# Attention and feed-forward block on one core: VectorE exps in groups of four tiles, an immediate exp bias, and measured times in the schedule model

## Chip, cores and metric

One NeuronCore of one Trainium2 chip. The metric is device time in microseconds (us) of one execution. Runs of one kernel agree within about 1.5% (the kernel before, over all its rounds: 1047.93 to 1064.23 us); every timed run here is in the fast state, except one single look, which has no state of its own and is marked. Ratios are the mean time of one kernel's runs over the mean of the kernel before's runs of the same rounds, so they are not quite the ratio of the medians that are quoted beside them.

Engine names in the profile: PE is TensorE (PEld its weight loads), ACT is ScalarE, DVE is VectorE, POOL is GpSimd.

## The reference

A pre-layernorm block: attention with 32 heads of width 16 over 2048 tokens of width 512, then a gated GELU layer of width 1792, both with residuals.

```python
q, k, v = split((layernorm(x) @ wqkv))           # 32 heads, Dh = 16
p = softmax(q @ k.T * Dh ** -0.5)                # 32 x 2048 x 2048 exps
h = x + (p @ v) @ wo
out = h + (gelu(layernorm(h) @ w_gate) * (layernorm(h) @ w_up)) @ w_down
```

The exps are the bulk: 2048 score tiles of 128 x 512.

## The kernel before

The program is built by a list scheduler that runs while the kernel is built. Every piece of work is an `Op` with an engine, a modelled duration, what it reads and what it writes. The scheduler keeps a modelled clock for each engine, always emits the op that can start first, and so fixes the **order** of instructions on each engine. On the chip, engines run their lists in that order and wait on semaphores. A wrong duration in the model costs no correctness; it gives an order in which an engine stands at an instruction whose input is late.

Attention runs in 40 units of four heads by 512 (in the last 16 units, 256) queries, with 64 (or 32) score tiles each. Q times K ("QK") fills PSUM banks 0 to 2 and 3 to 4 in turn. ScalarE turns three tiles and then two tiles into exps in the buffer `PT`. P times V ("PV") accumulates in bank 5. Banks 6 and 7 serve everything else: projections, the feed-forward layer, and score tiles whose exp VectorE computes instead of ScalarE.

```python
def _ready(self, op):                     # when the model lets an op start
    ...
    for k in op.reads:  r = max(r, self.done[P.last_writer[k]])
    ... # the same for the writers and readers of what it writes
    return r + LAT                        # LAT = 0.12, for every engine

def exps():                               # ScalarE, n = 3 or 2 tiles
    ...
    yield Op("act", 0.093 + 0.427 * n, ACTF(PT[:, p0:p0 + n, :], pbank[:, b0:b0 + n, :],
             ACT.Exp, scale=LN2 / 1024, bias=ebias[:]), ...)   # ebias: a 128x1 tile

def dexp(i, dn, b):                       # VectorE, one tile of 512 columns; [...] cut
    yield Op("dve", 0.66, tensor_scalar(out=X, in0=pbank[:, b, :], ...))   # conversion, frees the bank
    sch.release(b)
    yield Op("dve", 0.2,  tensor_scalar(out=M, in0=X, ...))    # mantissa
    yield Op("dve", 0.2,  tensor_scalar(out=E, in0=X, ...))    # power of two
    yield Op("dve", 0.33, tensor_tensor(out=W, in0=M, in1=M))
    yield Op("dve", 0.2,  tensor_scalar(out=W, in0=W, EK, EB))
    yield Op("dve", 0.33, tensor_tensor(out=W, in0=W, in1=M))
    yield Op("dve", 0.33, tensor_tensor(out=T, in0=W, in1=E))  # T; exp is E + T, by two matmuls

def pv():                                 # one step: four tiles, in order m = 0, 1, 2, ...
    for m in range(NT // r):
        yield Wait(lambda: all(4 * n + g in made for g in range(4)))
        ... # PE: PV of all four tiles; a VectorE tile takes two matmuls, with E and with T
```

## Time and profile before

Median of the first three runs 1058.76 us (1055.49 to 1060.64). From the ScalarE records I split the span as follows. "Exps" is the number of exps times their shortest start-to-start interval (1.423 us for three tiles, 0.997 for two). "Tanh" is 42 x 0.520 + 14 x 0.306. "Lost" is what remains between the first exp's start and the last exp's end. (Up to ten of the 256-wide tanhs start after the last exp, five of them in the kernel before, so "lost" is too low by up to 3 us.)

| us | head | exps | tanh | lost | tail after the last exp | span |
|---|---|---|---|---|---|---|
| before | 20.1 | 890.2 | 26.1 | 71.3 | 49.4 | 1057.0 |

From the page of the kernel before: busy time of each engine with its share of the span, then the costliest groups (line, engine, operation, tile written from tiles read, shapes, count; busy us, mean ns of one; idle time before them and what ended most of it).

```profile
PE 906.1 (86%) x7249; PEld 282.6 (27%) x7249; DVE 845.0 (80%) x1988; ACT 950.9 (90%) x830; POOL 200.0 (19%) x265
...
L1201 ACT ACTIVATE PT<-pbank,ebias 128x1536 bf16<-128x1536 f32 x736 | 912.5, 1398 | 51.8 <-PE pbank L1195 50.2
...
L1448 DVE TENSOR_SCALAR dX<-pbank 128x512 uint16<-128x512 f32 x208 | 142.2, 684 | 13.2 <-PE pbank L1195 12.7
...
L1455 DVE TENSOR_TENSOR dW<-dW,dM 128x512 f16<-128x512 f16 x208 | 102.1, 491 | 6.2
```

ScalarE is the busiest engine that cannot be relieved by waiting less: 912.5 of its 951 us are exps. (In a mixed group the shape named is the first one; the 736 exps are 368 of 1536 and 368 of 1024 columns.) VectorE spends seven instructions on each of 208 tiles, about 640 us.

The list of waits of the same kernel: who waited for whom, us in total, times, longest.

```profile
PEld pbank L1195 <- DVE dT L1457: 53.9, 85, 3.2
...
ACT PT L1201 <- PE pbank L1195: 50.2, 63, 3.1
PEld pbank L1194 <- DVE GUT L1630: 32.0, 30, 3.2
...
PE pbank L1195 <- DVE dT L1457: 25.1, 38, 2.7
```

PE stands 54 us at the weight load for `dT`, the last step of a VectorE exp, and ScalarE stands 50 us for PE. Three stretches of 50 us: busy time of each engine (with counts), the granted TensorE clock, DMA share, GB/s.

```profile
200.00:250.00 50.00, 43.34 (x311) 11.30 (x308) 45.77 (x124) 50.00 (x42) 0.00 (x0) 1.00 0.00 1
300.00:350.00 50.00, 40.54 (x255) 10.79 (x253) 40.96 (x71) 43.32 (x40) 26.25 (x25) 0.93 0.00 1
550.00:600.00 50.00, 37.36 (x207) 9.23 (x207) 44.46 (x76) 36.90 (x34) 23.64 (x23) 0.83 0.00 0
```

The first stretch has no feed-forward work (POOL at 0): ScalarE is busy without a gap. In the other two the feed-forward layer runs, and ScalarE falls to 43 and 37 of 50.

### The profile page before, as it was taken

To read this page: it belongs to the slowest core of one execution; us is meant where nothing else is said; L and a number is where in the kernel's file an instruction comes from. 1 tells how busy PE (TensorE), PEld (TensorE's weight loads), DVE (VectorE), ACT (ScalarE), POOL (GpSimd) and SP (SyncE) were. 2 spreads that over 40 slices of the span, in tenths; PEclk is the share of its full clock that TensorE was granted. 3 is DMA by queue.
4 is the path that set the end of the run, shared out by engine and by line. 5 is a ranking of instruction groups with operands and counts; after the bars stand their busy time and mean duration, and the time that the engine had idled before them with its cause. 6 is when DMAs were issued, how large, how long until landed. Compare 5 with 4: busy or idle time off the path is not lost.

```text
span 1057.0 us, 18656 instructions
## 1 busy us (share of the span) xinstructions
PE 906.1 (86%) x7249; PEld 282.6 (27%) x7249; DVE 845.0 (80%) x1988; ACT 950.9 (90%) x830; POOL 200.0 (19%) x265
## 2 busy tenths in 40 slices
PE   7999888888877799889887879988898878898877
PEld 2322222222212222222221222222233222333345
DVE  6457978998888989999778979999948898656853
ACT  6899999999988899999987888999999988999922
POOL 6300000000244410000033540000001454302340
PEclk8999999999999999999988899999999998999989
DMA  4000003200000001000000000100000000000000
GB/s 159 2 1 1 1 1 136 95 1 1 2 1 1 1 6 36 1 1 1 2 1 1 1 1 6 36 1 1 1 7 7 1 2 2 2 16 16 2 6 19
DMA packets 10769, 15.17 MB, mean 14 GB/s; under 512 B 688, under 2 KB 9136, under 8 KB 10672
## 3 DMA queue, kind: packets, MB, share of 16 engines
q1 hardware_dynamic: 10672, 13.90, 3.9%
q8 instruction: 59, 0.97, 0.4%
q14 instruction: 38, 0.31, 0.1%
HBM read 11.80 MB, written 2.10 MB: 13 GB/s over the span
## 4 chain that ended last, share of the span: by engine, by line
PE 28%; ACT 28%; DVE 28%; issue 14%; DMA 1%; SPq 0%; POOL 0%; ACTq 0%; DVEq 0%
ACT PT L1201 27%; PE pbank L1195 14%; PE pbank L1194 10%; DVE dW L1455 4%; PE pbank L1677 3%; DVE dT L1457 3%; DVE dX L1448 3%; DVE dW L1454 3%; DVE dW L1453 2%; DVE g_sb L1592 2%; DVE w_sb L1604 2%; DVE dM L1450 2%; DVE dE_57 L1451 2%; DVE QT L1332 2%; DVE GUT L1630 2%
## 5 line engine op out<-in xcount | busy, mean ns | idle before, releaser
L1201 ACT ACTIVATE PT<-pbank,ebias 128x1536 bf16<-128x1536 f32 x736 | 912.5, 1398 | 51.8 <-PE pbank L1195 50.2
L1195 PE MATMUL pbank<-QT,KT 32*128 32x512 bf16 (+1 forms) x2560 | 290.9, 344 | 74.5 <-ACT PT L1201 57.2
L1195 PE MATMUL pbank<-PT,VA 128*17 128x512 bf16 (+1 forms) x2312 | 206.2, 347 | 24.4 <-DVE dT L1457 21.7
L1195 PEld LDWEIGHTS pbank<-QT,KT 32*128 32x128 bf16 x2560 | 76.3, 91 | 353.6 <-ACT PT L1201 245.7
L1677 PE MATMUL pbank<-ones_bf,zero_bf 128*128 128x512 bf16 x483 | 153.7, 391 | 0.0
L1448 DVE TENSOR_SCALAR dX<-pbank 128x512 uint16<-128x512 f32 x208 | 142.2, 684 | 13.2 <-PE pbank L1195 12.7
L1555 POOL TENSOR_SCALAR rstd_105<-mv_104 128x1 f32<-128x1 f32 x16 | 3.8, 240 | 585.1 <-DVE mv_104 L1553 585.0
L1455 DVE TENSOR_TENSOR dW<-dW,dM 128x512 f16<-128x512 f16 x208 | 102.1, 491 | 6.2
L1457 DVE TENSOR_TENSOR dT<-dW,dE_57 128x512 bf16<-128x512 f16 x208 | 96.9, 466 | 6.0
L1594 POOL TENSOR_TENSOR w_sb<-g_sb 128x512 f32<-128x512 f32 (+1 forms) x56 | 56.6, 1011 | 213.2 <-DVE g_sb L1592 213.2
L1453 DVE TENSOR_TENSOR dW<-dM 128x512 f16<-128x512 f16 x208 | 90.5, 435 | 0.0
L1195 PEld LDWEIGHTS pbank<-PT,VA 128*17 128x17 bf16 x2312 | 52.5, 88 | 135.5 <-issue 64.4
L1195 PE MATMUL pbank<-dE_57,VA 128*17 128x512 bf16 (+1 forms) x248 | 82.2, 358 | 3.1 <-DVE dT L1457 3.1
L1195 PE MATMUL pbank<-dT,VA 128*17 128x512 bf16 (+1 forms) x248 | 81.7, 356 | 0.0
L1454 DVE TENSOR_SCALAR dW<-dW 128x512 f16<-128x512 f16 x208 | 71.9, 346 | 5.6
L1450 DVE TENSOR_SCALAR dM<-dX 128x512 uint16<-128x512 uint16 x208 | 67.6, 325 | 5.5
L1451 DVE TENSOR_SCALAR dE_57<-dX 128x512 uint16<-128x512 uint16 x208 | 68.2, 328 | 0.0
L1596 POOL TENSOR_TENSOR w_sb<-w_sb,g_sb 128x512 f32<-128x512 f32 (+1 forms) x56 | 67.1, 1198 | 4.7
L1677 PEld LDWEIGHTS pbank<-ones_bf,zero_bf 128*128 128x128 bf16 x483 | 39.3, 98 | 73.4 <-issue 62.2
L1194 PE MATMUL pbank<-wd_sb,GUT 128*128 128x512 bf16 x224 | 58.4, 382 | 0.2
L1592 DVE COPY g_sb<-pbank 128x512 f32<-128x512 f32 (+1 forms) x56 | 34.7, 620 | 20.7 <-PE pbank L1194 20.4
L1603 ACT ACTIVATE w_sb<-w_sb 128x512 f32<-128x512 f32 (+1 forms) x56 | 34.0, 607 | 13.3 <-POOL w_sb L1596 13.2
(126 smaller groups left out, 766.3 us busy)
## 6 DMA issues: line engine op xcount, KB each, us to landing
xres<-in_A_x_dram SPq DMA_DIRECT2D x16, 128.0 KB, 2.2
out_dram<-out_sb SPq DMA_DIRECT2D x16, 128.0 KB, 1.7
wg_sb<-in_B_w_gate_dram SPq DMA_DIRECT2D x1, 1792.0 KB, 7.0
wu_sb<-in_B_w_up_dram SPq DMA_DIRECT2D x1, 1792.0 KB, 11.5
wd_sb<-in_B_w_down_dram SPq DMA_DIRECT2D x1, 1792.0 KB, 16.6
x_sb<-in_A_x_dram SPq DMA_DIRECT2D x3, 512.0 KB, 10.3
wqkv_sb<-in_A_wqkv_dram SPq DMA_DIRECT2D x2, 768.0 KB, 8.7
x_sb<-in_A_x_dram SPq DMA_DIRECT2D x2, 256.0 KB, 3.9
```

The lines of the kernel that those rows point to most:

```text
L1194: return lambda e: e.matmul(o, l, r, start=start, stop=stop)
L1195: return lambda e: e.matmul(o, l, r, start=start, stop=stop, tile_position=tile)
L1201: return lambda e: e.activation(out=o, in_=i, func=func, **kw)
L1448: yield Op("dve", 0.66, lambda e: e.tensor_scalar(out=X, in0=pbank[:, b, :], scalar1=1024.0 * CENTER, scalar2=0.0, op0=ALU.add, op1=ALU.ma ...
L1450: yield Op("dve", 0.2, lambda e: e.tensor_scalar(out=M.bitcast(U16), in0=X, scalar1=0x3ff, scalar2=0x3c00, op0=ALU.bitwise_and, op1=ALU.bi ...
L1451: yield Op("dve", 0.2, lambda e: e.tensor_scalar(out=E.bitcast(U16), in0=X, scalar1=3, scalar2=0x1f80, op0=ALU.logical_shift_right, op1=AL ...
L1453: yield Op("dve", 0.33, lambda e: e.tensor_tensor(out=W, in0=M, in1=M, op=ALU.mult), reads=[kM], writes=[kW])
L1454: yield Op("dve", 0.2, lambda e: e.tensor_scalar(out=W, in0=W, scalar1=EK, scalar2=EB, op0=ALU.mult, op1=ALU.add), reads=[kW], writes=[kW])
L1455: yield Op("dve", 0.33, lambda e: e.tensor_tensor(out=W, in0=W, in1=M, op=ALU.mult), reads=[kW, kM], writes=[kW])
L1457: yield Op("dve", 0.33, lambda e: e.tensor_tensor(out=T, in0=W, in1=E, op=ALU.mult), reads=[kW, kE], writes=[kT])
L1596: yield Op("pool", 1.27, lambda e: e.tensor_tensor(out=ws, in0=ws, in1=gs, op=ALU.mult), reads=[("w", i), ("g", i)], writes=[("w", i)])
L1677: fill_op = Op("pe", TMM, lambda e: e.matmul(pbank[:, PVB, :], zero_bf[:], ones_bf[:], start=False, stop=False, skip_group_check=True), re ...
```

## The change

Intent: let VectorE do its exps in groups of four tiles (2048 columns an instruction, fewer fixed costs), take their PV products out of the ordered PV steps so that PE never waits for one tile, drop the bias pointer of the exp, and put measured times and a truer readiness rule into the schedule model. The core of the diff, with cuts marked:

```diff
     def _ready(self, op):
...
+            if op.eng == "pe":                       # PE no longer lags behind PE
+                lag = LAT + (SLACK if op.writes[0] in SOFT else 0.0)
+                return max([self.done[t] + lag for t in toks if t[0] != "pe"] + [0.0])
+            lag = LAT + (SLACK if op.eng == "act" and op.writes[0][0] == "w" else 0.0)
+            return max([self.done[t] + lag for t in toks] + [0.0])
...
+SLACK = 0.3
+SOFT = (("pb", 6), ("pb", 7))
-NRING = 25
+NRING = 20                                           # tiles in the ring PT
+GS = 4
+GLAST = 16
...
-    ... bias=ebias[:]
+    ... bias=-LN2 * (127 - CENTER) - math.log(EC)
...
+    def dconv(G, j, b):                              # once for each tile of a group
+        yield Op("dve", 0.7, ... tensor_scalar(out=dX[:, j, :], in0=pbank[:, b, :], ...
+    def dchain(G):                                   # once for each group, n tiles wide
+        t1, t2 = 0.16 + 0.133 * n, 0.16 + 0.267 * n
+        ... # three tensor_scalar of t1, three tensor_tensor of t2
...
     def pv():
+        # a group's products: one PE op, at any PV step of the unit once the group is done;
+        # the last PV step of a unit waits for all groups of the unit
```

A group may open only with at least 28 tiles (`GLAST + 12`) of the unit left, or in the last six tiles of the unit before, and only after the former group's chain has been issued but for its last instruction.

More of the change, by code (lines that the diff above doesn't have):

```diff
@@ L920, in _ready @@
         P = self.P
-        r = 0.0
+        toks = []
         for k in op.reads:
@@ L925, in _ready @@
                 return self.INF
-            r = max(r, self.done[tok])
+            toks.append(tok)
         if isinstance(op, Op):
@@ L930, in _ready @@
                 if tok is not None:
-                    r = max(r, self.done[tok])
-                for tok in P.readers.get(k, ()):
-                    r = max(r, self.done[tok])
-        return r + LAT
+                    toks.append(tok)
+                toks.extend(P.readers.get(k, ()))
+            if op.eng == "pe":
[3 more added lines that the diff above has]
+            return max([self.done[t] + lag for t in toks] + [0.0])
+        return max([self.done[t] + LAT for t in toks] + [0.0])
     def owed(self, t, n=0):
@@ L1035 @@
 F16, U16 = mybir.dt.float16, mybir.dt.uint16
-ND = 5
+GS = 4
+GLAST = 16
 DFROM = 20
-DGAP = 1.8
-DMAX = 8
+DGAP = 6.0
+DBUSY = 0.0
 LN2 = 0.6931471805599453
@@ L1103, in fast_path @@
     offX = cur[0]
-    dX = at("dX", [128, 2, 512], U16)
-    dM = at("dM", [128, 2, 512], F16)
-    dW = at("dW", [128, 2, 512], F16)
-    dE2 = at("dE2", [128, ND, 512], BF16)
-    dT = at("dT", [128, ND, 512], BF16)
-    ebias = at("ebias", [128, 1], FP32)
+    dX = at("dX", [128, GS, 512], U16)
+    dW = at("dW", [128, 2, GS, 512], F16)
+    dE2 = at("dE2", [128, 2, GS, 512], BF16)
     gset = at("gset", [128, 1], FP32)
@@ L1180, in fast_path @@
     TILES = [(u, m, g) for u in range(NU) for m in range(NT * CHUNKS[units[u][0]] // 512) for g in range(4)]
-    STEPS, own, made, acount = [], {}, set(), [0]
+    STEPS, own, made, groups = [], {}, set(), {}
     TUNIT = 0.88 * 64 * (0.093 * len(SLOTS) / sum(n for _, n in SLOTS) + 0.427)
     T0 = 12.0
+    unit0 = [sum(4 * NT * CHUNKS[c] // 512 for c, _ in units[:u]) for u in range(NU + 1)]
     sch = Sched(P, list(DENSE))
-    C = dict(exp=0, pv=0, oa=0, ln1=0, proj=0, oproj=0, gut=0, down=0, act=0, dbank=None, din=0, dn=0, dcons=0, dnext=0.0)
+    C = dict(exp=0, pv=0, oa=0, ln1=0, proj=0, oproj=0, gut=0, down=0, act=0, dbanks=[], gopen=None, gk=0, gw=0, gpv=0, acons=0, qpos=0, dnext=0.0)
     otok_n = {}
@@ L1227, in consts @@
         yield Op("pool", 0.1, lambda e: e.memset(zero_bf[:], 0.0), writes=["zero_bf"])
-        yield Op("pool", 0.1, lambda e: e.memset(ebias[:], -LN2 * (127 - CENTER) - math.log(EC)), writes=["ebias"])
         yield Op("pool", 0.3, lambda e: e.tensor_copy(out=ident32[:], in_=ident[:]), reads=["ident"], writes=["ident32"])
@@ L1358, in ffn_loads, with unit_of, pos_of @@
             yield Op("sp", 1.75, lambda e, o=o, i=i: e.dma_start(out=o, in_=i), writes=[nm], dma=nm, extra=lambda: dF)
+    def unit_of(i):
+        return TILES[i][0]
+    def pos_of(i):
+        u = unit_of(i)
+        return i - unit0[u], unit0[u + 1] - unit0[u]
     def qk():
-        nxt, an, dn = 0, 0, 0
+        nxt, an = 0, 0
         while nxt < len(TILES):
@@ L1365, in qk @@
             b0, n = SLOTS[st % len(SLOTS)]
-            n = min(n, len(TILES) - nxt)
-            STEPS.append((an, n, b0, nxt))
-            put = [(nxt + k, b0 + k) for k in range(n)]
-            for k in range(n):
-                own[nxt + k] = ("a", (an + k) % NRING)
-                acount.append(acount[-1] + 1)
-            nxt, an = nxt + n, an + n
-            d = None
-            db = C["dbank"]
-            if db is not None and nxt < len(TILES) - 12 and all(sch.done[t] <= sch.now + 0.7 for t in P.readers.get(("pb", db), ())):
-                d = (nxt, dn)
-                put.append((nxt, db))
-                own[nxt] = ("d", dn % ND)
-                acount.append(acount[-1])
-                nxt, dn = nxt + 1, dn + 1
-                C["dbank"] = None
+            mine = []
@@ new lines, in qk @@
+            while len(mine) < n and nxt < len(TILES):
+                if nxt not in own:
+                    own[nxt] = ("a", (an + len(mine)) % NRING)
+                    mine.append(nxt)
+                nxt += 1
+            STEPS.append((an, mine, b0))
+            put = [(i, b0 + k) for k, i in enumerate(mine)]
+            an += len(mine)
+            while nxt in own:
+                nxt += 1
+            C["qpos"] = nxt
+            G, late = C["gopen"], []
+            if G:
+                if nxt < len(TILES) and G["u"] is None and pos_of(nxt)[1] - pos_of(nxt)[0] >= GLAST + 12:
+                    G["u"] = unit_of(nxt)
+                used = {TILES[i][2] for i in mine}
+                while C["dbanks"] and len(G["t"]) < GS and len(put) < 4 and G["u"] is not None:
+                    db = C["dbanks"][0]
+                    if any(sch.done[t] > sch.now + 0.7 for t in P.readers.get(("pb", db), ())):
+                        break
+                    cand = [i for i in range(nxt, min(unit0[G["u"] + 1] - 8, nxt + 8)) if i not in own and TILES[i][2] not in G["g"] | used]
+                    if not cand:
+                        break
+                    i = cand[0]
+                    C["dbanks"].pop(0)
+                    own[i] = ("d", G["k"] % 2)
+                    late.append((i, len(G["t"]), db))
+                    G["t"].append(i)
+                    G["g"].add(TILES[i][2])
+                    used.add(TILES[i][2])
+                    put.append((i, db))
+                while nxt in own:
+                    nxt += 1
+                if len(G["t"]) == GS or nxt >= len(TILES) or (G["u"] is not None and (unit_of(nxt) != G["u"] or pos_of(nxt)[1] - pos_of(nxt)[0] <= GLAST)):
+                    close_group()
@@ L1396, in qk, with close_group @@
             C["qk"] = st + 1
-            if d:
-                sch.add(dexp(*d, db), 70000)
+            C["qpos"] = nxt
+            for i, j, db in late:
+                sch.add(dconv(G, j, db), -2)
         C["qkdone"] = 1
-        if C["dbank"] is not None:
-            sch.release(C["dbank"])
+        if C["gopen"]:
+            close_group()
+    def close_group():
+        G = C["gopen"]
+        C["gopen"] = None
+        for b in C["dbanks"]:
+            sch.release(b)
+        C["dbanks"] = []
+        if G["t"]:
+            groups.setdefault(G["u"], []).append(G)
+            sch.add(dchain(G), 70000)
+        else:
+            C["gk"] -= 1
     def exps():
@@ L1407, in exps @@
                 yield Wait(lambda: st < len(STEPS))
-            an, n, b0, i0 = STEPS[st]
-            p0 = an % NRING
-            yield Op("act", 0.093 + 0.427 * n, ACTF(PT[:, p0:p0 + n, :], pbank[:, b0:b0 + n, :], ACT.Exp, scale=LN2 / 1024, bias=ebias[:]),
-                     reads=[("pb", b0 + k) for k in range(n)] + ["ebias"], writes=[("PT", p0 + k) for k in range(n)],
-                     gate=lambda: C.get("qk", 0) >= st + 1 and acount[4 * C["pv"]] >= an + n - NRING)
+            an, mine, b0 = STEPS[st]
+            p0, n = an % NRING, len(mine)
+            yield Op("act", 0.093 + 0.427 * n, ACTF(PT[:, p0:p0 + n, :], pbank[:, b0:b0 + n, :], ACT.Exp, scale=LN2 / 1024, bias=-LN2 * (127 - CENTER) - math.log(EC)),
+                     reads=[("pb", b0 + k) for k in range(n)], writes=[("PT", p0 + k) for k in range(n)],
+                     gate=lambda: C.get("qk", 0) >= st + 1 and C["acons"] >= an + n - NRING)
             st += 1
             C["exp"] = st
-            made.update(range(i0, i0 + n))
+            made.update(mine)
         C["expdone"] = 1
@@ L1422, in dget, with room @@
     def dget():
+        def room():
+            if C["gopen"] or C["proj"] < DFROM or C["gw"] < C["gk"] or C["gk"] - C["gpv"] >= 2 or sch.t["dve"] > sch.now + 0.8:
+                return False
+            p, n = pos_of(min(C["qpos"], len(TILES) - 1))
+            if 6 < n - p < GLAST + 12 or C["qpos"] > len(TILES) - 30:
+                return False
+            busy = any(isinstance(s.head, Acquire) and s.head.reads and sch._ready(s.head) < sch.INF for s in sch.streams)
+            return sch.now >= C["dnext"] + (DBUSY if busy else 0)
@@ L1424, in dget @@
         while True:
-            sd.prio = 80000
-            yield Wait(lambda: "qkdone" in C or C["dbank"] is None and C["din"] < 2 and C["proj"] >= DFROM and sch.t["dve"] <= sch.now + 0.8
-                       and C["dn"] - C["dcons"] < ND and sch.now >= C["dnext"])
+            yield Wait(lambda: "qkdone" in C or room())
             if "qkdone" in C:
                 return
-            b = yield Acquire(gate=urge)
-            if "qkdone" in C:
-                sch.release(b)
-                return
@@ L1434, in dget @@
-            C["dbank"] = b
-            C["din"] += 1
-            C["dn"] += 1
-            C["dnext"] = sch.now + DGAP
-    def urge():
-        sd.prio = -3 if sch.now >= C["dnext"] + DMAX else 80000
-        return True
-    def dexp(i, dn, b):
-        d, x = dn % ND, dn % 2
-        X, M, W, E, T = dX[:, x, :], dM[:, x, :], dW[:, x, :], dE2[:, d, :], dT[:, d, :]
-        kX, kM, kW, kE, kT = ("dX", x), ("dM", x), ("dW", x), ("dE", d), ("dT", d)
-        yield Op("dve", 0.66, lambda e: e.tensor_scalar(out=X, in0=pbank[:, b, :], scalar1=1024.0 * CENTER, scalar2=0.0, op0=ALU.add, op1=ALU.max), reads=[("pb", b)], writes=[kX])
-        sch.release(b)
-        yield Op("dve", 0.2, lambda e: e.tensor_scalar(out=M.bitcast(U16), in0=X, scalar1=0x3ff, scalar2=0x3c00, op0=ALU.bitwise_and, op1=ALU.bitwise_or), reads=[kX], writes=[kM])
-        yield Op("dve", 0.2, lambda e: e.tensor_scalar(out=E.bitcast(U16), in0=X, scalar1=3, scalar2=0x1f80, op0=ALU.logical_shift_right, op1=ALU.bitwise_and), reads=[kX], writes=[kE],
-                 gate=lambda: C["dcons"] >= dn - ND + 1)
-        yield Op("dve", 0.33, lambda e: e.tensor_tensor(out=W, in0=M, in1=M, op=ALU.mult), reads=[kM], writes=[kW])
-        yield Op("dve", 0.2, lambda e: e.tensor_scalar(out=W, in0=W, scalar1=EK, scalar2=EB, op0=ALU.mult, op1=ALU.add), reads=[kW], writes=[kW])
-        yield Op("dve", 0.33, lambda e: e.tensor_tensor(out=W, in0=W, in1=M, op=ALU.mult), reads=[kW, kM], writes=[kW])
-        C["din"] -= 1
-        yield Op("dve", 0.33, lambda e: e.tensor_tensor(out=T, in0=W, in1=E, op=ALU.mult), reads=[kW, kE], writes=[kT])
-        made.add(i)
@@ new lines, in dget @@
+            G = C["gopen"] = dict(u=None, t=[], g=set(), k=C["gk"], conv=0)
+            C["gk"] += 1
+            C["dnext"] = sch.now + DGAP
+            while C["gopen"] is G:
+                yield Wait(lambda: C["gopen"] is not G or (len(G["t"]) + len(C["dbanks"]) < GS and len(C["dbanks"]) < 2))
+                if C["gopen"] is not G:
+                    break
+                b = yield Acquire()
+                if C["gopen"] is not G:
+                    sch.release(b)
+                    break
+                C["dbanks"].append(b)
@@ new lines, in dconv @@
+    def dconv(G, j, b):
+        yield Op("dve", 0.7, lambda e: e.tensor_scalar(out=dX[:, j, :], in0=pbank[:, b, :], scalar1=1024.0 * CENTER, scalar2=0.0, op0=ALU.add, op1=ALU.max),
+                 reads=[("pb", b)], writes=[("dX", j)])
+        sch.release(b)
+        G["conv"] += 1
+    def dchain(G):
+        d, n = G["k"] % 2, len(G["t"])
+        X, W, E = dX[:, 0:n, :], dW[:, d, 0:n, :], dE2[:, d, 0:n, :]
+        M, T = X.bitcast(F16), W.bitcast(BF16)
+        kX, kW, kE = [("dX", j) for j in range(n)], [("dW", d)], [("dE", d)]
+        t1, t2 = 0.16 + 0.133 * n, 0.16 + 0.267 * n
+        yield Wait(lambda: G["conv"] == n)
+        yield Op("dve", t1, lambda e: e.tensor_scalar(out=E.bitcast(U16), in0=X, scalar1=3, scalar2=0x1f80, op0=ALU.logical_shift_right, op1=ALU.bitwise_and), reads=kX, writes=kE,
+                 gate=lambda: C["gpv"] >= G["k"] - 1)
+        yield Op("dve", t1, lambda e: e.tensor_scalar(out=X, in0=X, scalar1=0x3ff, scalar2=0x3c00, op0=ALU.bitwise_and, op1=ALU.bitwise_or), reads=kX, writes=kX)
+        yield Op("dve", t2, lambda e: e.tensor_tensor(out=W, in0=M, in1=M, op=ALU.mult), reads=kX, writes=kW)
+        yield Op("dve", t1, lambda e: e.tensor_scalar(out=W, in0=W, scalar1=EK, scalar2=EB, op0=ALU.mult, op1=ALU.add), reads=kW, writes=kW)
+        yield Op("dve", t2, lambda e: e.tensor_tensor(out=W, in0=W, in1=M, op=ALU.mult), reads=kW + kX, writes=kW)
+        C["gw"] += 1
+        yield Op("dve", t2, lambda e: e.tensor_tensor(out=T, in0=W, in1=E, op=ALU.mult), reads=kW + kE, writes=kW)
+        G["done"] = 1
@@ L1460, in pv, with prod @@
     def pv():
         n = 0
+        started = set()
+        def prod(i, tiles):
+            u, m, g = TILES[i]
+            c, slot = units[u]
+            nq = CHUNKS[c]
+            r = 512 // nq
+            out = []
+            for e in range(r):
+                for tl in tiles:
+                    kt = m * r + e
+                    out.append((len(out), MM(pbank[32 * g:32 * g + 17, PVB, 0:nq], VA[:, kt, head(slot, g), :], tl[:, e * nq:e * nq + nq], (u, g) not in started, m == NT // r - 1 and e == r - 1, (0, 32 * g))))
+                    started.add((u, g))
+            return out
@@ L1465, in pv @@
             r = 512 // nq
-            for m in range(NT // r):
-                yield Wait(lambda: all(4 * n + g in made for g in range(4)))
-                fns, rd, late = [], [], []
-                nd = 0
-                for e in range(r):
-                    kt = m * r + e
-                    for g in range(4):
-                        kind, p = own[4 * n + g]
-                        src = [(PT, "PT")] if kind == "a" else [(dE2, "dE"), (dT, "dT")]
-                        for j, (tl, key) in enumerate(src):
-                            f = MM(pbank[32 * g:32 * g + 17, PVB, 0:nq], VA[:, kt, head(slot, g), :], tl[:, p, e * nq:e * nq + nq], kt == 0 and j == 0, kt == NT - 1 and j == len(src) - 1, (0, 32 * g))
-                            (late if j else fns).append(f)
-                            rd.append((key, p))
-                        nd += kind == "d"
-                yield Op("pe", TPV + 0.05 * (r - 1) + 0.1 * min(1, nd), cols=512 + 128 * nd // r, fns=fns + late,
-                         reads=[("V", kt) for kt in range(m * r, m * r + r)] + ["VA_ones"] + sorted(set(rd)), writes=[("pb", PVB)],
-                         gate=lambda: C["oa"] >= u)
+            nm = NT // r
@@ new lines, in pv @@
+            for m in range(nm):
+                ts = [4 * n + g for g in range(4)]
+                yield Wait(lambda: all(i in own and (own[i][0] == "d" or i in made) for i in ts) and
+                           (m < nm - 1 or ((not C["gopen"] or C["gopen"]["u"] != u) and all("done" in G for G in groups.get(u, ())))))
+                for G in groups.get(u, ()):
+                    if "done" in G and "pv" not in G and m:
+                        d = G["k"] % 2
+                        fns = []
+                        for j, i in enumerate(G["t"]):
+                            fns += prod(i, [dE2[:, d, j, :], dW[:, d, j, :].bitcast(BF16)])
+                        fns = [f for _, f in sorted(fns, key=lambda a: a[0])]
+                        kts = sorted({TILES[i][1] * r + e for i in G["t"] for e in range(r)})
+                        yield Op("pe", 2 * TPV + 0.1 * (r - 1), cols=256 * len(G["t"]), fns=fns, reads=[("V", kt) for kt in kts] + ["VA_ones", ("dE", d), ("dW", d)], writes=[("pb", PVB)],
+                                 gate=lambda: C["oa"] >= u)
+                        G["pv"] = 1
+                        C["gpv"] += 1
+                ta = [i for i in ts if own[i][0] == "a"]
+                if ta:
+                    fns = []
+                    for i in ta:
+                        fns += prod(i, [PT[:, own[i][1], :]])
+                    fns = [f for _, f in sorted(fns, key=lambda a: a[0])]
+                    yield Op("pe", TPV + 0.05 * (r - 1), cols=128 * len(ta), fns=fns,
+                             reads=[("V", kt) for kt in range(m * r, m * r + r)] + ["VA_ones"] + [("PT", own[i][1]) for i in ta], writes=[("pb", PVB)],
+                             gate=lambda: C["oa"] >= u)
@@ L1483, in pv @@
                 n += 1
                 C["pv"] = n
-                C["dcons"] = 4 * n - acount[4 * n]
-                C["open"] = m + 1 < NT // r
+                C["acons"] += len(ta)
+                C["open"] = m + 1 < nm
             sch.add(ofin(u), -1.0)
```

## The prediction

> **What bounds it now.** ScalarE's exps. The page shows ACT busy 951 of 1057 us, 912.5 of it in 736 exps (368 of 1536 and 368 of 1024 columns). Stretches of 50 us without feed-forward work (200-250, 450-500, 700-750) show ACT busy 49.7 to 50.0. From the ACT records, first exp at 20.1 us, last end at 1007.6: 20 us of head, 49 of tail, 988 in which exps set the pace. Start to start, back-to-back exps take 1.423 and 0.997 us, so 736 cost 891 us; tanhs add about 26; some 71 us are idle or lost. The losses sit in feed-forward stretches (300-400, 550-650, 850-900: ACT 37 to 44 of 50). There the list of waits shows ACT behind PE (50 us in all), and PE behind the last step of a VectorE exp (dT, 54 us at the weight load, 25 at the matmul) and behind GUT evacuations.
>
> **ScalarE, immediate bias.** Start to start, an exp costs its columns at 0.833 ns plus 143 ns; a tanh followed directly by an exp costs 520 ns for 512 columns and 306 for 256, i.e. columns plus 93. The tanh has no pointer operand, the exp a bias pointer. So the change should save 50 ns an exp: 1.373 and 0.947 us. The Trainium skill, "ScalarE: Activation LUTs" (speed of the ACTIVATE instruction), puts a pointer operand at about 93 ns; this trace supports 50 back to back, which I use. 733 exps times 50 ns = 37 us, all on the critical path.
>
> **VectorE.** One exp tile now costs 3.08 us on VectorE (means: conversion 0.684, then 0.325, 0.328, 0.435, 0.346, 0.491, 0.466). 208 of 2048 tiles take 640 of its 845 busy us. In fours: four conversions 2.74, three 2048-wide tensor-scalars about 0.7 each, three tensor-tensors about 1.25 each (estimates: the 512-wide ones have minima near 0.28 and 0.42, of which 0.13 and 0.27 scale with width). Sum 8.6 us, 2.15 a tile, 30% less. The page "VectorE: DVE Perf Modes" (the perf-mode tier table) gives 0.69 and 1.22 us for 2048 elements, which agrees with that estimate.
> But the count is set by scheduling: a group opens only with more than 28 tiles of the unit left or in its predecessor's last six, and only after the former group's chain is issued, about 10 us with bank waits. That gives some two groups per 64-tile unit, one per 32-tile unit: about 216 tiles (170 to 260), as now. So VectorE's saving (175 us) mostly becomes slack. Ten tiles more or fewer are worth 4.6 us.
>
> **TensorE.** Products of VectorE tiles leave the in-order sequence of PV steps, so waits on dT should mostly vanish (79 us of PE waiting now, little of it reaching ACT). New: the last PV step of a unit waits for its groups; the ring of PT falls from 25 to 20. PE's work is unchanged except fill (154 us now), and it has slack. Later matmuls into banks 6 and 7 in the model should cut GUT waits. I give these together 21 us of the 71.
>
> **Sum.** 1832 ACT tiles = 733 exps at 1.160 = 850; tanh 26; idle 50; head 20; tail 49: 995 us. Range 962 to 1028. Faster by over 2%: 0.88; within 2%: 0.10; slower: 0.02.
>
> **What would show it.** Exp starts 1.373/0.947 us apart; VectorE tiles 170 to 260; VectorE busy falling towards 680; PE waits on the group product below 30 us; ACT idle before exps below 40.
>
> **What would make it wrong.** The pointer's 50 ns hidden or larger; groups far more frequent (to 960) or starved; groups' long VectorE ops (1.2 us) delaying evacuations in feed-forward stretches, or unit ends stalling PV until the ring is full, so that idle grows.

## The result

The changed kernel is correct and takes 966.84 us (median of 4, 965.93 to 969.95), beside 1057.12 for the kernel before (median of 4): ratio 0.9154, 95% interval 0.911 to 0.9199. The forecast said 995, range 962 to 1028: the time is inside, near the lower end.

| us | head | exps | tanh | lost | tail | span | ScalarE tiles | VectorE tiles |
|---|---|---|---|---|---|---|---|---|
| before | 20.1 | 890.2 | 26.1 | 71.3 | 49.4 | 1057.0 | 1840 | 208 |
| predicted | 20 | 850 | 26 | 50 | 49 | 995 | 1832 | 216 |
| after | 18.9 | 840.9 | 26.1 | 40.3 | 38.0 | 964.2 | 1883 | 165 |

The same groups on the page of the changed kernel:

```profile
PE 861.9 (89%) x7131; PEld 285.0 (30%) x7257; DVE 629.8 (65%) x973; ACT 900.3 (93%) x847; POOL 219.8 (23%) x264
...
L1206 ACT ACTIVATE PT<-pbank 128x1536 bf16<-128x1536 f32 x753 | 863.5, 1314 | 15.8 <-PE pbank L1200 15.1
...
L1496 DVE TENSOR_SCALAR dX<-pbank 128x512 uint16<-128x512 f32 x165 | 111.1, 687 | 122.7 <-PE pbank L1200 122.1
...
L1516 DVE TENSOR_TENSOR dW<-dW,dE_56 128x2048 bf16<-128x2048 f16 (+3 forms) x46 | 55.6, 1209 | 1.0
```

The exps are 17 more (753) and yet 49 us less busy. A VectorE product is now one instruction for a whole group. VectorE has fallen from 845 to 630 us, so it has slack. The waits:

```profile
ACT PT L1206 <- PE pbank L1200: 15.1, 24, 3.7
...
ACT w_sb L1687 <- POOL w_sb L1680: 14.5, 16, 1.9
...
PEld pbank L1200 <- DVE dW L1516: 8.2, 14, 1.2
...
PEld pbank L1199 <- DVE GUT L1714: 6.4, 15, 1.0
...
PE pbank L1200 <- DVE dW L1516: 3.3, 5, 0.9
```

PE's wait for the last VectorE step has gone from 54 to 8 us, for GUT at the weight load from 32 to 6, and ScalarE's wait for PE from 50 to 15. The three stretches (the feed-forward work of the second one now lies at 500):

```profile
200.00:250.00 50.00, 44.24 (x336) 13.20 (x339) 35.91 (x48) 49.72 (x45) 0.00 (x0) 1.00 0.00 1
300.00:350.00 50.00, 44.43 (x296) 13.48 (x297) 38.46 (x52) 46.76 (x47) 29.30 (x26) 1.00 0.00 1
500.00:550.00 50.00, 44.41 (x285) 12.78 (x290) 40.07 (x53) 45.23 (x45) 35.41 (x30) 0.97 0.00 1
```

In the first stretch ScalarE does 45 exps where it did 42. In the feed-forward stretches it now reaches 47 and 45 of 50.

### The profile page after: what moved, and what is told of

Read it like the earlier page. It is cut to its first block, busy times and chain, and to the rows that moved or that the text cites. A ratio compares the mean times of both kernels' runs of the same rounds, so it can differ in the third digit from the quotient of the medians.

```text
span 964.2 us, 17572 instructions
## 1 busy us (share of the span) xinstructions
PE 861.9 (89%) x7131; PEld 285.0 (30%) x7257; DVE 629.8 (65%) x973; ACT 900.3 (93%) x847; POOL 219.8 (23%) x264
## 4 chain that ended last, share of the span: by engine, by line
ACT 39%; PE 31%; issue 16%; POOL 7%; DVE 5%; DMA 1%; SPq 0%; ACTq 0%; DVEq 0%; POOLq 0%
ACT PT L1206 38%; PE pbank L1200 15%; PE pbank L1199 10%; PE pbank L1761 4%; POOL w_sb L1680 3%; POOL w_sb L1678 2%; POOL w_sb L1679 2%; ACT w_sb L1687 1%; DMA x_sb<-in_A_x_dram 1%; PE pbank L1203 1%; DVE g_sb L1676 1%; DVE w_sb L1688 1%; DVE OA L1581 1%; DVE dX L1496 0%; DVE dX L1511 0%
## 5 line engine op out<-in xcount | busy, mean ns | idle before, releaser
L1206 ACT ACTIVATE PT<-pbank 128x1536 bf16<-128x1536 f32 x753 | 863.5, 1314 | 15.8 <-PE pbank L1200 15.1
L1496 DVE TENSOR_SCALAR dX<-pbank 128x512 uint16<-128x512 f32 x165 | 111.1, 687 | 122.7 <-PE pbank L1200 122.1
L1688 DVE SCALAR_TENSOR_TENSOR w_sb<-w_sb,g_sb 128x512 f32<-128x512 f32 (+1 forms) x56 | 45.9, 820 | 18.0 <-ACT w_sb L1687 17.7
L1516 DVE TENSOR_TENSOR dW<-dW,dE_56 128x2048 bf16<-128x2048 f16 (+3 forms) x46 | 55.6, 1209 | 1.0
L1514 DVE TENSOR_TENSOR dW<-dW,dX 128x2048 f16<-128x2048 f16 (+3 forms) x46 | 53.6, 1164 | 1.1
L1512 DVE TENSOR_TENSOR dW<-dX 128x2048 f16<-128x2048 f16 (+3 forms) x46 | 52.5, 1140 | 1.2
L1687 ACT ACTIVATE w_sb<-w_sb 128x512 f32<-128x512 f32 (+1 forms) x56 | 34.6, 619 | 15.0 <-POOL w_sb L1680 14.5
L1679 POOL TENSOR_SCALAR w_sb<-w_sb 128x512 f32<-128x512 f32 (+1 forms) x56 | 46.9, 838 | 4.9
L1714 DVE SCALAR_TENSOR_TENSOR GUT<-pbank,w_sb 128x512 bf16<-128x512 f32 (+1 forms) x56 | 34.6, 618 | 10.6 <-PE pbank L1199 10.1
L1199 PE MATMUL pbank<-xnT,wqkv_sb 128*128 128x512 bf16 x121 | 34.1, 381 | 3.8 <-DVE QT L1336 2.7
L1581 DVE COPY OA<-pbank 128x512 f32<-128x512 f32 (+1 forms) x40 | 23.2, 580 | 20.5 <-PE pbank L1200 20.5
```

What stands on the lines that cost most here:

```text
L1199: return lambda e: e.matmul(o, l, r, start=start, stop=stop)
L1206: return lambda e: e.activation(out=o, in_=i, func=func, **kw)
L1496: yield Op("dve", 0.7, lambda e: e.tensor_scalar(out=dX[:, j, :], in0=pbank[:, b, :], scalar1=1024.0 * CENTER, scalar2=0.0, op0=ALU.add, o ...
L1512: yield Op("dve", t2, lambda e: e.tensor_tensor(out=W, in0=M, in1=M, op=ALU.mult), reads=kX, writes=kW)
L1514: yield Op("dve", t2, lambda e: e.tensor_tensor(out=W, in0=W, in1=M, op=ALU.mult), reads=kW + kX, writes=kW)
L1516: yield Op("dve", t2, lambda e: e.tensor_tensor(out=T, in0=W, in1=E, op=ALU.mult), reads=kW + kE, writes=kW)
```

## The experiments

Twelve kernels ran, each beside the kernel before on the same chip; all were correct. Each list of terms is worked out as in the tables above. All, in one table (the time is the median of 4 runs; "VE" is the number of VectorE tiles; `e9` is a single look):

| run | what it is | time | ratio [95%] | exps | lost | tail | VE |
|---|---|---|---|---|---|---|---|
| (after) | the change | 966.8 | 0.9154 [0.911, 0.920] | 840.9 | 40.3 | 38.0 | 165 |
| e1_old_imm | before + immediate bias | 1025.7 | 0.9694 [0.965, 0.974] | 821.7 | 109.5 | 50.3 | 208 |
| e3_old_imm_times | e1 + VectorE times in the model | 1003.5 | 0.9515 [0.946, 0.957] | 836.5 | 70.3 | 50.5 | 175 |
| e4b_old_imm_ready | e1 + readiness rule | 999.9 | 0.9426 [0.938, 0.947] | 822.4 | 94.9 | 36.9 | 207 |
| e4_old_imm_times_ready | e1 + both | 972.6 | 0.9182 [0.915, 0.922] | 834.6 | 54.6 | 36.9 | 181 |
| e8_old_times_ready_ptr | e4 with the pointer | 1021.0 | 0.9651 [0.960, 0.970] | 902.5 | 34.6 | 36.6 | 181 |
| e5_new_oldready | after, old readiness rule | 1015.8 | 0.9595 [0.956, 0.963] | 844.2 | 62.1 | 62.9 | 159 |
| e2_new_ptr | after with the pointer | 1017.7 | 0.9612 [0.958, 0.964] | 910.2 | 21.6 | 38.3 | 165 |
| e9_new_twoptr | after, bias and scale pointers | 1081.5 | (one look) | 980.2 | 16.5 | 38.2 | 165 |
| e6_new_nodve | after without VectorE exps | 1026.8 | 0.9698 [0.966, 0.974] | 915.4 | 28.9 | 34.2 | 0 |
| e7_new_act05 | after, ScalarE's exp re-measured in the model | 966.1 | 0.912 [0.908, 0.916] | 840.9 | 38.8 | 38.9 | 166 |
| e10_twin_dx | after, groups may overlap | 971.3 | 0.9211 [0.916, 0.927] | 831.6 | 52.5 | 36.9 | 186 |
| e11_twin_dx_open | e10, groups open more often | 977.4 | 0.9269 [0.922, 0.932] | 820.8 | 70.0 | 38.3 | 210 |

### The bias alone, and the bias taken back

```diff
# e1: the kernel before, with
-    bias=ebias[:]
+    bias=-LN2 * (127 - CENTER) - math.log(EC)        # and the memset of ebias gone
# e2: the changed kernel, with the opposite edit
```

> The kernel before with the immediate bias alone (and the memset of the bias tile gone); instruction order otherwise as before, 736 exps, 208 VectorE tiles. Theory P (a pointer operand costs 93 ns back to back, as the changed kernel's 1330/903 ns against 1423/997 show): starts 1330 and 903 ns apart, 736 x 93 ns = 68 us, so about 989 us (0.935), and the rest of the change is worth only about 22 us. Theory of the prediction (50 ns): 1020 us (0.965). Theory Q (the old order cannot feed a faster ScalarE because PE waits on VectorE's last step): 1005 to 1020 us, pitch 1330/903, but more idle before exps than the 52 us of before.

> The changed kernel with the bias read from a 128x1 tile again, all else as changed. Theory P: starts 1423 and 997 ns apart, 753 x 93 ns = 70 us more than 967, about 1037 us (0.98 of before). If a slower ScalarE merely eats the idle time of the changed kernel (40 us lost), less: 1000 to 1020.

Starts in e1 are 1.330 and 0.903 us apart, in e2 1.422 and 0.995: the pointer costs 93 ns an exp in both orders, not the 50 of the prediction. Yet e1 took 1025.7 us, close to what 50 ns would have given. The time alone would have confirmed the wrong figure. The terms tell it apart: exps fell by 68.5 us as 93 ns say, and lost time rose from 71.3 to 109.5. So theory Q of the expectation held. The waits of e1, to be read against those of before:

```profile
PEld pbank L1195 <- DVE dT L1456: 83.1, 142, 3.2
ACT PT L1201 <- PE pbank L1195: 73.2, 110, 3.8
...
PE pbank L1195 <- DVE dT L1456: 36.6, 69, 2.7
```

PE now waits 83 us for `dT` instead of 54, and ScalarE 73 us for PE instead of 50. In the old order more than half of a faster ScalarE was given back as waits. In the new order the pointer is worth 51 of 70 us (1017.7 against 966.8): here too lost time takes up the rest (21.6 against 40.3).

### Each pointer by itself

```diff
# e9: the changed kernel, with
-    scale=LN2 / 1024, bias=-LN2 * (127 - CENTER) - math.log(EC)
+    scale=escale[:], bias=ebias[:]                   # two 128x1 tiles
```

> The changed kernel with both the bias and the scale of the exp read from 128x1 tiles. If each pointer operand costs 93 ns back to back: starts 1330 + 186 = 1516 and 904 + 186 = 1090 ns apart. If only the first pointer costs: 1423 and 997, as in e2. Time about 967 + 2 x 51 = 1070 us in the first case.

Starts are 1.515 and 1.088 us apart: 1280 or 853 ns for the columns plus 235. With one pointer it was 143, with none 50. Each pointer operand adds 93 ns (92.5 for the second). A tanh followed by such an exp still starts 0.519 to 0.520 us before it, so the pointer's cost lies with the instruction that has it. The time, 1081.5 us, is 11 over what I expected, because less lost time was left to absorb it (16.5 us).

### The schedule model without the groups

```diff
# e4: the kernel before with the immediate bias (as e1), and
-    return r + LAT
+    (the new rule of _ready, SLACK and SOFT, as in the change)
-    dexp: 0.66, 0.2, 0.2, 0.33, 0.2, 0.33, 0.33
+    dexp: 0.7, 0.29, 0.29, 0.43, 0.29, 0.43, 0.43    # us in the model only
# e3: e4 without the new rule.  e4b: e4 with the old VectorE times.
# e8: e4 with the bias pointer.
```

> No groups: single VectorE exps, their products inside the ordered PV step as before, ring of 25, but with immediate bias, the new readiness rule of the schedule model, and measured VectorE times in the model (0.7, 0.29, 0.43 us). 181 VectorE tiles. Theory M (after the bias, what the change gained is the truer schedule model, not the groups): 970 us or less. Theory G (the groups and their free-standing products matter: PE still waits on the last VectorE step): 985 us or more, with PE waits on that step above 40 us.

> As e4 (no groups, immediate bias, new readiness rule), but the model keeps its old VectorE times (0.66, 0.2, 0.33 us); 207 VectorE tiles instead of 181. If the readiness rule is what counts: within 10 us of e4's 973. If the true VectorE times count (VectorE was overbooked, so PE waited on its last step): 985 to 1010, PE waits on that step near the 120 us of e1 rather than the 56 of e4, although ScalarE has 26 tiles (12 us) less to do.

> e4 without the new readiness rule: no groups, immediate bias, measured VectorE times in the model; 175 VectorE tiles. With e4 (973), e5 (1016, groups under the old rule) and the changed kernel (967) it completes a square of readiness rule by groups. If the rule is worth as much without groups as with them (49 us): about 1022. If the VectorE times alone had repaired the old order: 985 or less.

> e4 with the bias pointer back: the model's part of the change alone, without bias and groups; 181 VectorE tiles, starts 1423/997 ns apart. From e4's 747 exps x 93 ns = 69 us, less what the slower ScalarE takes back of e4's 55 us of lost time (the changed kernel lost 40 us, and 22 us with the pointer): 1015 to 1030. If bias and model help each other strongly (the pointer's time hides nearly all that the model saves): 1045 or more.

e4, which has no group at all, took 972.6 us, 2.6 over the bound that I had set for theory M (970) and 12 under that of theory G (985). The waits on `dT` are 39 us (56 in the counting of the expectation, above the 40 of theory G), but they cost little time. The ratio's interval, 0.9148 to 0.9217, overlaps that of the whole change. So the groups are worth some 9 us at most on top of the rest (an estimate from the widths of the two intervals); whether they are worth anything in time is not settled by these runs. The waits of e4, to be read against those of the change:

```profile
PEld pbank L1201 <- DVE dT L1462: 39.2, 62, 1.6
ACT PT L1207 <- PE pbank L1201: 34.3, 48, 3.4
...
ACT w_sb L1608 <- POOL w_sb L1601: 3.5, 9, 1.1
```

They show why so little is left over. With groups ScalarE waits 19 us less for PE (15.1 against 34.3) but 11 us more for GpSimd's part of the gate, in front of a tanh (14.5 against 3.5), and it has 16 tiles more to do (181 VectorE tiles in e4, 165 in the change: 7 us by ScalarE's time).

The two halves of the model are both needed. True VectorE times alone take e1 from 1025.7 to 1003.5 (e3). The rule alone takes it to 999.9 (e4b). Both take it to 972.6. The waits show which half does what; here those of e4b and of e3:

```profile
PEld pbank L1201 <- DVE dT L1462: 95.2, 157, 2.2
ACT PT L1207 <- PE pbank L1201: 66.4, 89, 2.7
...
PE pbank L1201 <- DVE dT L1462: 44.1, 76, 2.1
```

```profile
ACT PT L1201 <- PE pbank L1195: 41.5, 75, 3.0
...
PEld pbank L1195 <- DVE dT L1456: 32.0, 43, 2.4
...
PE pbank L1195 <- DVE dT L1456: 18.1, 22, 2.1
```

With the old VectorE times (e4b) the model believes that a VectorE exp takes 2.25 us (the sum of the seven figures) where it takes 3.08, books 207 of them, and PE waits 95 us for their last step. With the true ones (e3) it books 175, and the wait is 32 us. The rule's own mark is the tail: 49.4, 50.3, 50.5 and 62.9 us in the four kernels with the old rule (before, e1, e3, e5), 34.2 to 38.9 in all ten with the new one. In the trace of before, gate and up work of the chunk before last runs on for some 18 us after the last exp; in the changed kernel for some 9. The expectation for e3 (1022 if the rule is worth as much without groups as with them) missed by 19 us: without groups the rule is worth 31 us, with them 49.

e8 was within its range: bias and model without groups save 3.1% (e1) and 3.5% (e8) singly, and 8.2% together (e4). They help each other: with the pointer back, the order of e4 loses 34.6 us, without it 54.6; the old order loses 71.3 and 109.5.

### The groups under the old rule

```diff
# e5: the changed kernel, with
-    (the new rule of _ready)
+    return r + LAT                                   # for every engine, as before
```

> The changed kernel with the old readiness rule in the schedule model (PE ops again lag behind PE ops, no slack on banks 6 and 7); groups and immediate bias kept; 159 VectorE tiles against 165. Theory M: clearly slower than 967, 990 us or more. Theory G: within 10 us of 967.

It took 1015.8 us: theory M again. Under the old rule the groups are 12 us worse than the single exps of e3 (1003.5; the intervals just touch), under the new rule 6 us better than those of e4, and that difference is inside the intervals.

### What the VectorE tiles are worth, and how many

```diff
# e6: -DFROM = 20       +DFROM = 999                  # no VectorE exps
# e10: +dX doubled, a group may open while the former one is in its chain
#      -NRING = 20      +NRING = 15                   # to make room
# e11: e10, and GLAST 16 -> 12, "+ 12" -> "+ 6", DGAP 6 -> 0,
#      VectorE queue limit for opening 0.8 -> 3 us
```

> The changed kernel with no VectorE exps at all: 2048 tiles on ScalarE, 819 exps x 1.117 us = 915 us against 841. If the 165 tiles save what ScalarE would spend on them: 967 + 74 = 1041 us, less up to 20 us of waits that go with them: 1020 to 1041. If the groups' waits eat most of their gain: below 1000.

> The changed kernel with two buffers for the conversions, so that a group may open while the one before is still in its chain; the ring of PT goes from 20 to 15 to make room. 186 VectorE tiles against 165: 21 tiles x 0.447 us = 9 us less on ScalarE. If each tile moved to VectorE is worth its ScalarE time: about 958. If the added groups' work returns as waits (VectorE tiles near the balance in feed-forward stretches, or the shorter ring): 965 or slower.

> As e10, with groups allowed later in a unit (12 and 6 tiles instead of 16 and 12), no minimum gap and a deeper VectorE queue: 210 VectorE tiles, about the 216 of the prediction. ScalarE has 45 tiles x 0.447 = 20 us less to do than in the changed kernel: 947 us if all of it lands. If the count of groups does not matter any more, because ScalarE's lost time grows by as much: 960 to 970.

Without VectorE exps the kernel takes 1026.8 us: the 165 tiles are worth 60 us, 0.36 us a tile, against 0.447 of ScalarE time (1.117 us for 2.5 tiles); lost time is 28.9 without them and 40.3 with them. From there on the exchange turns bad. At 186 tiles ScalarE has 9.3 us less to do and loses 12.2 more; at 210 tiles it has 20.1 us less to do and loses 29.7 more. e10 and e11 take 4 and 11 us more than the change (the interval of e10 overlaps the change's, that of e11 does not). The ring was cut as well, and groups open at other places, so the count is not the only difference; but the expected gain of a tile, 0.447 us, plainly no longer lands.

Where it goes shows in a feed-forward stretch of e11, first the busy times, then some rows of VectorE and GpSimd in order of time (start, length, engine, line, operation):

```profile
500.00:550.00 50.00, 38.69 (x250) 12.00 (x256) 41.98 (x56) 36.51 (x37) 38.39 (x34) 0.97 0.00 1
```

```profile
520.22 1.55 DVE L1513 TENSOR_SCALAR dW<-dW 128x2048 f16<-128x2048 f16 x1
...
523.88 1.03 POOL L1678 TENSOR_TENSOR w_sb<-g_sb 128x512 f32<-128x512 f32 x1
523.91 2.08 DVE L1514 TENSOR_TENSOR dW<-dW,dX 128x2048 f16<-128x2048 f16 x1
...
527.53 1.69 DVE L1516 TENSOR_TENSOR dW<-dW,dE 128x2048 bf16<-128x2048 f16 x1
```

ScalarE is at 36.5 of 50 where the changed kernel has 45.2. A 2048-wide tensor_scalar takes 1.55 us and tensor_tensors 2.08 and 1.69 us beside GpSimd's work on the gate. In the stretch from 200 to 250 of the changed kernel, where GpSimd is idle, the same instructions take:

```profile
L1514 DVE TENSOR_TENSOR dW<-dW,dX 128x2048 f16<-128x2048 f16 x4 | 4.9, 1223 | 0.1
...
L1513 DVE TENSOR_SCALAR dW<-dW 128x2048 f16<-128x2048 f16 x4 | 2.8, 692 | 0.1
```

The Trainium skill, "SBUF — State Buffer" (section "SBUF: two separate sides"), says that GpSimd and VectorE share a port pair as an exclusive lock held for a whole instruction, with the other one blocked, when the VectorE instruction runs in a two-port mode or has two SBUF inputs. The trace agrees as far as it goes: 1.22 us alone, up to 2.08 beside GpSimd; it shows the slowing, not the lock. GpSimd pays as well. Its tensor_scalar on the gate, first in e6, which has no VectorE exps, then in the changed kernel:

```profile
L1679 POOL TENSOR_SCALAR w_sb<-w_sb 128x512 f32<-128x512 f32 (+1 forms) x56 | 39.5, 705 | 4.9
```

```profile
L1679 POOL TENSOR_SCALAR w_sb<-w_sb 128x512 f32<-128x512 f32 (+1 forms) x56 | 46.9, 838 | 4.9
```

The mean goes from 705 to 838 ns. GpSimd's three instructions on the gate take 162 us together in e6, in the kernel before and in e4, and 183 us in the change, so the price is already there in the change. It does not rise further: 182 us in e10 and 183 in e11. So this contention does not explain by itself why lost time grows in e10 and e11. What grows most is ScalarE's wait for PE, from 15.1 us in the change to 26.9 in e10 and, with its wait for GpSimd, to these in e11:

```profile
ACT PT L1206 <- PE pbank L1200: 33.4, 36, 3.5
...
ACT w_sb L1687 <- POOL w_sb L1680: 19.3, 21, 3.2
```

What holds PE up there (the longer VectorE chains, the shorter ring or the later groups) no run isolates.

### ScalarE's time in the model

```diff
# e7: -    yield Op("act", 0.093 + 0.427 * n, ...      +    yield Op("act", 0.05 + 0.427 * n, ...
```

> The changed kernel with ScalarE's exp put into the schedule model as it is measured now, 0.050 us plus 0.427 a tile instead of 0.093; 166 VectorE tiles. If a truer model again shortens the waits: 940 to 960 us, lost time of ScalarE below 35 us. Rival (the model's surplus of 43 ns an exp is a useful margin): 967 or slower.

It took 966.1 us, the same as the change: the rival held. Correcting a model by 43 ns an exp on the engine that is the bottleneck anyway gave nothing, while correcting the engines that feed it gave the larger part of the gain (e1 to e4). No version of mine beats the changed kernel clearly.

## Why the prediction was right, point by point

**Right in kind.** ScalarE's exps bound the kernel before and after; VectorE's saving became slack (845 to 630 us busy); VectorE's cost a tile was sized well (2.15 us forecast, 2.24 in the records: 369 us for 165 tiles); PE's waits on the last VectorE step nearly vanished (54 to 8 us, or 79 to 11.5 in the prediction's counting, below the 30 that I named); idle before exps fell below 40 (51.8 to 15.8).

**The size of the pointer.** The step that failed is "this trace supports 50 back to back, which I use": it is 93 ns. This alone is worth 0.043 us x 733 = 32 us of the 31 by which the forecast was too high. I had compared an exp (PSUM source, bias pointer) with a tanh (SBUF source, no pointer). Two things differed, and the second one hid 43 ns: in the changed kernel, where neither has a pointer, the exp starts the next one after its columns plus 50 ns, and the tanh still after its columns plus 93. The right control was in the trace of before all the time: two copies from PSUM without a pointer, at the start of the kernel.

```profile
11.39 1.07 ACT L1297 ACTIVATE xnT<-pbank 128x512 bf16<-128x512 bf16 x2
...
12.73 0.60 ACT L1297 ACTIVATE xnT<-pbank 128x512 bf16<-128x512 bf16 x1 [0.28 <-PE pbank L1292]
```

Two copies back to back end 1.07 us after the first one's start, though one alone takes 0.60: in the records the second starts 0.478 us after the first, 427 ns for 512 columns plus 51. The Trainium skill, "ScalarE: Activation LUTs" (section "What ACT_TABLE_LOAD costs"), gives 93 ns for a pointer operand; the runs agree, and I had set it aside for a measurement of something else.

**The number of tiles.** I said about 216 (170 to 260); it was 165, outside the range. My count, two groups in every 64-tile unit and one in every 32-tile unit, held where there is no feed-forward work (16 conversions in the stretch from 200 to 250), not where there is (7 from 500 to 550) nor in the last two chunks. That the feed-forward layer keeps the two banks is my reading of it, not tested. By ScalarE's time that is 51 x 0.447 = 23 us too optimistic. But e11, with 210 tiles, is slower than the change: beyond the change's 165 a tile no longer brought its ScalarE time.

**Idle and tail.** I gave groups and model 21 us of the 71 lost; it was 31. The tail fell by 11 us, which I had not foreseen; e5 and the old-rule kernels tie it to the readiness rule. The errors sum: -32 (pointer) + 23 (tiles) - 10 (lost) - 11 (tail) - 1 (head) = -31, which is 995 to 964. Two large errors partly cancelled, so that the total came this close is partly luck.

**The cause, as the prediction put it.** The 37 us for the bias were to lie "all on the critical path". Put into the old kernel alone, the true 68 us gave 33 (e1). And the largest part of the gain, which I had put last and sized together with the groups at 21 us, is the schedule model: from e1 to e4 the ratio falls from 0.9694 to 0.9182. Along the path before, e1, e3, e4, after, the ratios are 1, 0.9694, 0.9515, 0.9182, 0.9154: bias 3.1% of the time before, VectorE times 1.8%, readiness rule 3.3%, groups 0.3%. In another order the shares differ, since they help each other.

**Open.** Which part of the rule counts, PE's lag behind itself, the slack on banks 6 and 7 or the slack before ScalarE's work on the gate, no run tells. Whether groups are faster than single exps at all under the new rule is inside the intervals. A rival that no run isolates is the granted TensorE clock, which is lower in the stretches where ScalarE loses time (0.93 and 0.83 before, 1.00 and 0.97 after). It cannot carry the model's gain: the profiled runs of e1 and e4 have 0.976 and 0.983, and if all of TensorE's work slowed in proportion, that would be some 7 us (an estimate) of the 53 between them. From e4 to the change (0.983 to 0.996) the same estimate gives some 12 us, more than the 6 between them, so it is one more reason to leave the groups' worth open.

## What to carry to other kernels

When a bottleneck engine is made faster, ask first whether the others' order can feed it: split the span into its busy terms, lost time and tail, and judge an experiment by the term, since a total can agree with a wrong figure. A static schedule's wrong durations are a cost like any other, and here those of the engines that feed the bottleneck mattered more than its own. When you read a fixed cost from two groups of a trace, see that they differ in one thing only, source memory included.

## What the Trainium skill lacked or had wrong

- "ScalarE: Activation LUTs": it gives 186 ns plus 0.833 ns a column for an activation without pointers, and an overlap of about 93 ns back to back, so 93 ns plus the columns from start to start. From PSUM the runs show 50 ns plus the columns (1.330 us for 1536, 0.903 for 1024, 0.477 for 512), from SBUF 93 (0.519 for 512, 0.305 for 256). It is the fixed cost that differs, not the overlap: in the kernel before, a 512-wide copy in bf16 takes 577 ns from PSUM with the next start after 478, and 619 from SBUF (this one with an accumulator output; a tanh has the same figures) with the next start after 519. That page gives one fixed cost for both sources; the skill has the two elsewhere, in the errata table of "VectorE: DVE Perf Modes" (for ScalarE 224 cycles from SBUF and 172 from PSUM at 1.2 GHz, 43 ns apart), and the runs agree. Its 93 ns a pointer held: 50, 143, 235 ns with none, one, two.
- "VectorE: DVE Perf Modes": its 693 and 1224 ns for 2048 elements held to 2 ns with GpSimd idle (692 to 694, 1223 to 1226). The table gives no figure beside a busy GpSimd; here up to 1.55 and 2.08 us.
